# Chunk-selected attention with a squared-ReLU FFN: from single heads with the FFN in blocks to head pairs with the FFN spread in

## The chip, the cores and the metric

The kernel runs on one core of a Trainium2 chip. The metric is the time of one execution on the device, in microseconds (us), lower is better. Engines are named as in the profile: PE is the matrix engine, PEld its weight loads, DVE the vector engine, ACT the scalar engine, POOL the general one, SP the one that issues the stores. PSUM is the memory that PE writes its sums to. The kernel before took 596.76 us (median of the four runs beside which the changed kernel was timed, 593.55 to 600.3).

## The reference

Four batches of 8 heads, 768 positions, 64 columns per head. Keys come in 24 chunks of 32. A query may look at the six chunks with the highest upper bound, which is computed from each chunk's smallest and largest key values, and only backwards. The result of attention, 3072 tokens by 512, goes through an FFN.

```python
k_min, k_max = min and max of k over each chunk of 32
ub = np.sum(np.maximum(q * k_min, q * k_max), axis=-1)      # [.., S, 24]
ub = np.where(causal, ub, -1e9)
top_chunks = np.argsort(ub, axis=-1)[..., -6:]
scores = scale * q @ k.T                                     # masked by chunk and causality
attn = np.exp(scores - max); attn = attn / sum
x = (attn @ v), heads side by side                           # [3072, 512]
h = np.maximum(x @ w_in, 0.0)                                # [3072, 2048]
return h * h @ w_out                                         # [3072, 512]
```

## The kernel before

Work is done head by head. Each head's q and k are transposed on PE; the bounds, the six best and a mask row per chunk are made in steps of 128 queries. The mask rows are appended to q and k (64 + 24 rows), so the score matmul adds the mask. Values go through 65-column matmuls (64 values and a column of ones for the sum), one per 128 queries. The FFN of batches 0 and 1 runs in blocks between the heads of batches 2 and 3; that of batches 2 and 3 runs at the end.

```python
# all weights are loaded first, then q, k, v of a whole batch, as rows of 64 values
nc.gpsimd.dma_start(out=w_in_sb, in_=...)          # ... w_out_sb likewise
nc.gpsimd.dma_start(out=qn, in_=q[b].rearrange("h (j p) d -> p (h j) d", p=128))

def ffn_up(tb, f):                                 # [cut: the loop below is whole]
    ph = psB.tile([128, TOKB], F32, tag="po", name="ph")     # same buffers as the value sums
    for ki in range(NKI):
        nc.tensor.matmul(ph, lhsT=w_in_sb[:, ki, 128*f:128*(f+1)],
                         rhs=xT_sb[:, ki, TOKB*tb:TOKB*(tb+1)], ...)
    # [cut: relu on ACT, square on DVE]
# ffn_down: py from the same psB buffers, 16 matmuls of 512 columns

# per head:
for i in range(NT):                                # bounds and choice, 128 queries at a time
    nc.tensor.matmul(ub_p, lhsT=qr_comb[:, 128*i:128*(i+1)], rhs=kmm, ...)
    nc.vector.tensor_add(ubm, ub_p, ubmask[...])
    nc.vector.max(out=m8, in_=ubm)
    nc.vector.tensor_scalar(selb, ubm, m8[:, 5:6], 0.0, op0=ALU.subtract, op1=ALU.min)
    nc.tensor.matmul(selbT_p[...], lhsT=selb, rhs=ident, is_transpose=True, ...)
nc.scalar.copy(qs_comb[D:KC, :], selbT_p)
for blk in range(NBLK):
    pouts = [psB.tile([128, D + 1], F32, tag="po") for _ in range(3)]
    for j in range(0, i_hi):
        nc.tensor.matmul(ps[:, :w], lhsT=kq_comb[0:KC, ...], rhs=qs_comb[0:KC, qs:q1], ...)
        nc.scalar.activation(e[:, :w], ps[:, :w], ACT.Exp)
        for i in range(max(j, i_lo), i_hi):        # values: 65 moving columns
            nc.tensor.matmul(pouts[ii], lhsT=e[:, col:col+128], rhs=v_aug[:, j, :], ...)
    # [cut: reciprocal of the sum, multiply, per 128 queries]
```

The softmax here doesn't subtract the row's maximum and nothing guards it: scores larger than these inputs give would overflow.

## Time and profile before

| stage of the kernel before | from, to (us) | what it is |
|---|---|---|
| wait | 0 to 32 | q queued behind 4 MB of weights |
| 16 heads without FFN | 32 to 235 | first preparation (to 50 us), then mostly 11.2 us per head, 22.4 per two |
| 16 heads with half of the FFN | 235 to 500 | 16.6 us per head, 33 per two |
| rest of the FFN | 500 to 597 | PE full |

The page of the kernel before: the first PE line is busy us with its share and count of instructions. In the rows by slice each digit stands for a fortieth of the span (14.9 us here), in tenths.

```profile
span 597.3 us, 7719 instructions
...
PE 467.0 (78%) x2592; PEld 227.8 (38%) x2592; DVE 287.6 (48%) x1280; ACT 285.0 (48%) x537; POOL 87.4 (15%) x223
...
PE   0037787787787778787878988789888889999997
...
PEclk9999999999999999955777778777687778999999
```

PE is busy in only 7 to 8 tenths of most slices, and the recorded clock (PEclk) starts at full speed and falls in the second half. The table by windows has the stages; the columns are those of its first line.

```profile
core 0: us, PE busy (x) PEld busy (x) DVE busy (x) ACT busy (x) POOL busy (x), PEclk, DMA share, GB/s
0.00:32.40 32.40, 0.03 (x1) 0.03 (x2) 0.00 (x0) 3.58 (x4) 10.00 (x18) 1.00 1.23 161
32.40:235.00 202.60, 148.50 (x925) 78.86 (x925) 126.94 (x586) 110.38 (x215) 50.56 (x111) 1.00 0.87 41
235.00:500.00 265.00, 224.80 (x1226) 106.31 (x1226) 137.94 (x633) 133.38 (x255) 26.89 (x95) 0.73 0.06 10
500.00:597.30 97.30, 93.71 (x443) 42.62 (x441) 22.77 (x61) 37.65 (x64) 0.00 (x0) 0.99 0.11 44
```

The clock column must be read with care: it shows 1.00 wherever the record of the clock is empty, and here the record begins only at 251 us. There is a second meter in the trace: the mean time of a score matmul of 384 columns. The Trainium skill, "TensorE: Matmul & The Clock Gate", section "Single matmul latency", gives (219 + N)/1.2 ns at the half clock and (398 + N)/2.4 ns at the full one, so for N = 384 an estimate of about 502 and 326 ns. The traces agree: single ones take about 0.50 or 0.33 us; a mean between is a mixture of both. The profile models the ends of matmuls, so the meter was checked against starts: six transposes in a row take 0.85 us in the stage without FFN (at 38.43 us) and 0.52 us after a block of FFN (at 290.75 us). Here is the group in 60 to 80 us and in 320 to 340 us of the kernel before (count, then busy us and mean ns of one):

```profile
L275 PE MATMUL ps<-qs_comb,kq_comb 88*128 88x384 bf16 x10 | 4.8, 508 | 0.0
...
L275 PE MATMUL ps<-qs_comb,kq_comb 88*128 88x384 bf16 x5 | 2.2, 472 | 0.9 <-ACT qs_comb L262 0.9
```

So the whole stage without FFN ran at half clock, whatever the row PEclk says, and even among the FFN blocks most of the attention did (in 20 us windows the mean goes between 389 and 510 ns).

The chain that ended last, and the groups that the change touches (busy us, mean ns; then the idle time before them):

```profile
PE 59%; DVE 16%; ACT 12%; DMA 5%; issue 3%; POOL 3%; ACTq 0%; POOLq 0%; DVEq 0%
...
L289 PE MATMUL po<-vn,e 128*128 128x65 bf16 x672 | 104.5, 242 | 12.0 <-ACT e L280 4.7
L111 PE MATMUL ph<-xT_sb,w_in_sb 128*128 128x512 bf16 x384 | 108.1, 446 | 3.6 <-DVE x_sb L297 3.6
```

PE has 59% of the chain, but DVE and ACT, with their small operations, 28%.

### The profile page before, as it was taken

What the parts mean: (1) busy time and instruction counts of PE and PEld (TensorE: products, weight loads), DVE (VectorE), ACT (ScalarE), POOL (GpSimd) and SP (SyncE); (2) the same over time, 40 slices, a digit from 0 to 9 for tenths busy, and PEclk for the clock granted to TensorE, in tenths of its full rate; (3) what the DMA queues carried; (4) which work ended last, traced back from release to release, by engine and by line L of the source; (5) the groups of instructions that cost most, each with busy time, mean ns of one, the idle gap of its engine ahead of it and who ended that gap; (6) DMA issues with size and microseconds to landing.
All of it is one profiled execution on the core that took longest, in us unless ns stands there. A gap on an engine that the chain in (4) does not pass through costs nothing.

```text
span 597.3 us, 7719 instructions
## 1 busy us (share of the span) xinstructions
PE 467.0 (78%) x2592; PEld 227.8 (38%) x2592; DVE 287.6 (48%) x1280; ACT 285.0 (48%) x537; POOL 87.4 (15%) x223
## 2 busy tenths in 40 slices
PE   0037787787787778787878988789888889999997
PEld 0023343343344334443333434333344434444443
DVE  0036656656755666766555343564327541514040
ACT  2025556455556465555556445554445441526261
POOL 6033114113114112111001011000110110000000
PEclk9999999999999999955777778777687778999999
DMA  7999107909004909000000000000000000010101
GB/s 135 187 147 125 5 2 50 57 0 55 0 1 28 79 2 53 1 2 0 2 0 2 18 36 18 2 0 19 18 36 0 2 1 36 36 53 19 53 19 70
DMA packets 80007, 20.41 MB, mean 34 GB/s; under 512 B 74336, under 2 KB 76384, under 8 KB 79968
## 3 DMA queue, kind: packets, MB, share of 16 engines
q0 software_dynamic: 76512, 13.63, 37.5%
q1 hardware_dynamic: 3456, 6.29, 2.7%
q8 instruction: 20, 0.33, 0.2%
q14 instruction: 19, 0.16, 0.1%
HBM read 27.26 MB, written 6.29 MB: 56 GB/s over the span
## 4 chain that ended last, share of the span: by engine, by line
PE 59%; DVE 16%; ACT 12%; DMA 5%; issue 3%; POOL 3%; ACTq 0%; POOLq 0%; DVEq 0%
PE ph L111 17%; PE py L125 15%; PE ps L275 9%; PE po L289 8%; ACT e L280 7%; DMA kn<-in_k_dram 5%; DVE selb L257 4%; PE kT_p L224 4%; PE qT_p L215 3%; ACT qr_comb L220 2%; DVE ubm L253 2%; DVE x_sb L297 2%; POOL e L282 2%; DVE kmm L232 2%; PE selbT_p L259 2%
## 5 line engine op out<-in xcount | busy, mean ns | idle before, releaser
L280 ACT ACTIVATE e<-ps 128x384 bf16<-128x384 f32 (+2 forms) x288 | 111.6, 418 | 63.2 <-PE ps L275 41.5
L275 PE MATMUL ps<-qs_comb,kq_comb 88*128 88x384 bf16 (+2 forms) x288 | 109.0, 419 | 15.9 <-ACT qs_comb L262 9.1
L289 PE MATMUL po<-vn,e 128*128 128x65 bf16 x672 | 104.5, 242 | 12.0 <-ACT e L280 4.7
L111 PE MATMUL ph<-xT_sb,w_in_sb 128*128 128x512 bf16 x384 | 108.1, 446 | 3.6 <-DVE x_sb L297 3.6
L282 POOL TENSOR_SCALAR_AFFINE_SELECT e<-e 128x128 bf16<-128x128 bf16 x192 | 54.3, 295 | 363.7 <-ACT e L280 362.0
L289 PEld LDWEIGHTS <-e 128*128 128x128 bf16 x672 | 58.4, 118 | 75.1 <-POOL e L282 27.3
L117 ACT ACTIVATE ht<-ph 128x512 bf16<-128x512 f32 x96 | 57.4, 597 | 47.8 <-PE ph L111 46.7
L296 DVE RECIPROCAL recip<-po 128x1 f32<-128x1 f32 x192 | 30.8, 164 | 80.1 <-PE po L289 73.7
L111 PEld LDWEIGHTS <-w_in_sb 128*128 128x128 bf16 x384 | 41.6, 111 | 62.0 <-issue 24.0
L259 PE MATMUL selbT_p<-ident,selb 128*24 128x128 bf16 x192 | 44.3, 260 | 19.2 <-DVE selb L257 11.7
L218 DVE COPY qs_comb<-qT_p 64x768 bf16<-64x768 bf16 x32 | 17.5, 548 | 82.1 <-PE qT_p L215 39.1
L215 PE MATMUL qT_p<-ident,qn 128*64 128x128 bf16 x192 | 25.3, 281 | 39.9 <-DMA qn<-in_q_dram 32.4
L220 ACT ACTIVATE qr_comb<-qT_p 64x768 bf16<-64x768 bf16 x32 | 25.7, 802 | 59.9 <-DVE qr_comb L219 59.5
L134 ACT COPY ob<-py 128x512 f32<-128x512 f32 x24 | 14.1, 586 | 72.8 <-PE py L125 69.9
L262 ACT COPY qs_comb<-selbT_p 24x768 bf16<-24x768 bf16 x32 | 25.0, 780 | 48.1 <-PE selbT_p L259 48.1
L249 PE MATMUL ub_p<-kmm,qr_comb 128*128 128x24 bf16 x192 | 32.3, 189 | 18.7 <-DVE ubm L253 17.0
L297 DVE TENSOR_SCALAR x_sb<-po,recip 128x64 bf16<-128x64 f32 x192 | 45.2, 274 | 1.0
L275 PEld LDWEIGHTS <-kq_comb 88*128 88x128 bf16 x288 | 33.4, 122 | 25.7 <-issue 21.4
L253 DVE TENSOR_TENSOR ubm<-ub_p,ubmask 128x24 f32<-128x24 f32 x192 | 32.1, 185 | 18.0 <-PE ub_p L249 16.2
L224 PE MATMUL kT_p<-ident,kn 128*64 128x128 bf16 x192 | 31.1, 286 | 11.1 <-DVE kmm L232 6.6
L259 PEld LDWEIGHTS <-selb 128*24 128x24 bf16 x192 | 16.5, 92 | 51.4 <-DVE selb L257 36.2
L215 PEld LDWEIGHTS <-qn 128*64 128x64 bf16 x192 | 18.3, 143 | 42.9 <-DMA qn<-in_q_dram 32.4
(699 smaller groups left out, 572.2 us busy)
## 6 DMA issues: line engine op xcount, KB each, us to landing
out_dram<-ob SPq DMA_DIRECT2D x24, 256.0 KB, 2.0
qn<-in_q_dram POOLq DMA_DIRECT2D x4, 768.0 KB, 10.7
kn<-in_k_dram POOLq DMA_DIRECT2D x4, 768.0 KB, 12.2
vn<-in_v_dram POOLq DMA_DIRECT2D x4, 768.0 KB, 10.8
w_in_sb<-in_moe_w_in_dram POOLq DMA_DIRECT2D x1, 2048.0 KB, 13.3
w_out_sb<-in_moe_w_out_dram POOLq DMA_DIRECT2D x1, 2048.0 KB, 21.8
```

The costliest lines, as they stand in the source:

```text
L111: nc.tensor.matmul(ph, lhsT=w_in_sb[:, ki, 128 * f:128 * (f + 1)], rhs=xT_sb[:, ki, TOKB * tb:TOKB * (tb + 1)], start=(ki == 0), stop=(ki ...
L117: nc.scalar.activation(ht, ph, ACT.Relu)
L125: nc.tensor.matmul(py, lhsT=h2state[(tb, f)][:, 128 * t:128 * (t + 1)], rhs=w_out_sb[:, f, :], start=(f == 0), stop=(f == NFI - 1))
L215: nc.tensor.matmul(qT_p[:, 128 * j:128 * (j + 1)], lhsT=qn[:, j, :], rhs=ident, is_transpose=True, start=(j == 0), stop=(j == NT - 1))
L224: nc.tensor.matmul(kT_p[:, 128 * j:128 * (j + 1)], lhsT=kn[:, j, :], rhs=ident, is_transpose=True, start=(j == 0), stop=(j == NT - 1))
L253: nc.vector.tensor_add(ubm, ub_p, ubmask[:, off:off + NC])
L259: nc.tensor.matmul(selbT_p[:, 128 * i:128 * (i + 1)], lhsT=selb, rhs=ident, is_transpose=True, start=(i == 0), stop=(i == NT - 1))
L275: nc.tensor.matmul(ps[:, :w], lhsT=kq_comb[0:KC, 128 * j:128 * (j + 1)], rhs=qs_comb[0:KC, qs:q1], start=True, stop=True)
L280: nc.scalar.activation(e[:, :w], ps[:, :w], ACT.Exp)
L282: nc.gpsimd.affine_select(out=e[:, 0:128], in_=e[:, 0:128], compare_op=ALU.is_ge, fill=0.0, base=0, channel_multiplier=-1, pattern=[[1, 128]])
L289: nc.tensor.matmul(pouts[ii], lhsT=e[:, col:col + 128], rhs=v_aug[:, j, :], start=(not started[ii]), stop=(j == i))
L297: nc.vector.tensor_scalar_mul(x_sb[:, NT * b + i, D * h:D * (h + 1)], pouts[ii][:, 0:D], recip)
```

## The change

Its intent: handle two heads at once so that the small per-128-query operations become wide ones; keep values and sums transposed, so that attention's output needs no transpose before the FFN; load q and k of one pair first, in long packets; and mix the FFN finely into the attention. Values and sums of the two heads go to the two halves of the array (64 columns each). The diff, cut to its core:

```diff
-    nc.gpsimd.dma_start(out=w_in_sb, ...)          # weights first
+    states = {0: load_qk(0)}                       # q and k of pair 0 first, weights with pair 1
+            nc.gpsimd.dma_start(
+                out=t, in_=src[b, 2 * hp:2 * hp + 2].rearrange(
+                    "h (p j) d -> p h j d", p=128))          # rows of 6 x 64 values
 ...
+            nc.vector.tensor_copy(tt.rearrange("d (p j) -> d p j", j=NT),
+                                  pt.rearrange("d (j p) -> d p j", j=NT))   # puts them in order
 ...
+        for i in range(NS):                        # bounds of both heads: block-diagonal kmx, kmn
+            nc.tensor.matmul(ub[:, i], lhsT=qp[:, cols], rhs=kmx[s], start=True, stop=False)
+            nc.tensor.matmul(ub[:, i], lhsT=qm[:, cols], rhs=kmn[s], start=False, stop=True)
+        nc.vector.tensor_add(ubm, ub, ubmask)      # all queries of both heads at once
 ...
-                nc.tensor.matmul(pouts[ii], lhsT=e[:, col:col + 128],
-                                 rhs=v_aug[:, j, :], ...)
+                    rows = slice(D * hh, D * hh + D)
+                    nc.tensor.matmul(av[rows, off:], lhsT=vn[:, hh, j, :], rhs=e[:, off:], ...)
+                    nc.tensor.matmul(den[rows, off:], lhsT=ones, rhs=e[:, off:], ...)
 ...
-            ph = psB.tile([128, TOKB], F32, tag="po", name="ph")
+            ph = psf.tile([128, QB], F32, tag="ff", name="ph")     # own buffers
 ...
+                if j > 0:
+                    values(j - 1)
+                run_ffn(per_step[0])               # one or two FFN units after each score step
+                per_step.append(per_step.pop(0))
 ...
+            nc.scalar.activation(rc, den, ACT.Ln)
+            nc.scalar.activation(rc, rc, ACT.Exp, scale=-1.0)
+            nc.vector.tensor_mul(xT[:, hp, S * b + q0:S * b + q1], av, rc)
```

The FFN of batch b now fills the pairs of batch b + 1; the first four of the 16 pairs have none, and a quarter of the FFN is left for the end.

## The prediction

> **What bounds the kernel now**, by stages of the 597 us execution (windows, chain of waits):
> - 0 to 32 us: the first transpose waits 32.4 us for q, queued behind 4 MB of weights in 256-byte packets.
> - 32 to 235: 16 heads without FFN, 11.2 us each. The page gives clock 1.00, but a 384-column score matmul takes 508 ns, as in the window recorded at 0.50 (505), so I take this stage as cold: the Trainium skill ("TensorE: Matmul & The Clock Gate", the two states) gives 1.2 GHz until the array has been busy for a few us. No engine is full; PE is near its cold limit.
> - 235 to 500: 16 heads, 16.6 us each, with half of the FFN in blocks between heads. The clock swings between 0.50 and 1.00 (mean about 0.72): FFN blocks warm the array, attention cools it.
> - 500 to 597: the other half, PE 100%, 216 ns per 512-column matmul: at its limit.
>
> **What the change does**, per pair of heads (estimates from durations in the trace):
> - PE: value matmuls of 65 columns become wide ones (5376 columns of values, 5376 of sums, 5376 of scores). 9.2 us warm, 17 cold, against 11 and 19. FFN unchanged: 164 us warm in all, 10.2 per pair. PE work hardly falls.
> - DVE: small operations per 128 queries (add 0.18, max 0.18, subtract 0.23, reciprocal 0.16, scale 0.27) give way to wide ones. Two reordering copies from PSUM at about 0.93, four reduces 0.94, ten max 0.18, small copies: 11.5 us against about 18; plus 2 with FFN.
> - ACT: exps 7.5 as before, mask rows and q/k copies gone (6.4), Ln and Exp of the sums added (1.9): 9.4 against 14; 14 with FFN. One table load.
> - The 96 transposes of x vanish.
> - Start: q/k of one pair alone, 1.5 KB packets: about 9 us, not 32, then one exposed preparation of 11.
> - FFN of batch b fills batch b+1: 3/4 rides under attention, 1/4 is tail.
>
> **Sum.** Start 20; four pairs without FFN, 17.5 each (cold PE): 70; twelve with FFN, PE-bound, 19.4 warm, at a mean clock of about 0.78: 25.5 each, 306; tail 2 x 21.7 plus the end: 47. **Predicted 443 us, 395 to 495 in 8 of 10.** Chances: faster by over 2% 0.96, within 2% 0.02, slower 0.02.
>
> **What would show it.** First transpose before 12 us. Pairs without FFN 15 to 20 us apart; with FFN 22 to 29. DVE busy about 230 us, ACT about 235. Clock in the FFN pairs above 0.75, PE over 90% busy there. Tail about 45 us at 216 ns per 512-column matmul. PE over 70% of the chain of waits.
>
> **What would make it wrong.**
> - The clock: if fine mixing keeps PE cold, FFN pairs cost up to 37 us (near 560 in all); if it stays warm, 21 (about 390).
> - Preparation of pair p+1 is one long DVE chain (7 us before the bounds, 2.4 more before the mask transpose). If it stalls PE instead of overlapping with the pair before, add up to 8 us per pair.
> - Sums and values have one PSUM buffer each: Ln, Exp, multiply (about 1.7 us) sit between blocks, twice per pair.
> - Half-array matmuls alternate with full ones. The skill ("TensorEngine Tiling (Array Packing)", Key Properties) says that a mode change drains the array; nothing in this trace prices it. Halves that overlap would save up to a quarter of the value work.
> - Reordering copies might be slower than 0.93 us.

## More of the kernel before

How the clock is lost is seen in the timeline of PE between two blocks (start, length, engine, line, operation, count, and the wait before it):

```profile
283.31 7.15 PE L111 MATMUL ph<-xT_sb,w_in_sb 128*128 128x512 bf16 x20 [0.44 <-DVE x_sb L297]
...
292.00 1.06 PE L259 MATMUL selbT_p<-ident,selb 128*24 128x128 bf16 x4
293.94 0.43 PE L275 MATMUL ps<-qs_comb,kq_comb 88*128 88x384 bf16 x2 [0.87 <-ACT qs_comb L262]
...
295.35 0.33 PE L275 MATMUL ps<-qs_comb,kq_comb 88*128 88x384 bf16 x1
...
295.54 0.50 PE L275 MATMUL ps<-qs_comb,kq_comb 88*128 88x384 bf16 x1
```

The clock has come up during a block of 20 FFN matmuls. Then come 3.5 us of transposes, tiny bound matmuls and waits. The score matmul at 295.35 still takes 0.33 us; the next, at 295.54, takes 0.50. The attention that follows runs at half clock until the next block.

## The result, and the profile after

The changed kernel is correct and took **380.78 us** (median of 4, 379.96 to 381.55) against 596.76 for the kernel before. The ratio is 0.6369, with a 95% interval from 0.6332 to 0.6406. Ratios here are the mean time of one kernel's fast runs over that of the other's of the same rounds, so not quite the ratio of the medians. The direction was right; the time is 62 us under the middle of the prediction and 14 under its lower end.

The page, and the windows of its stages (start; four pairs without FFN; twelve pairs with FFN; tail), with the columns as before:

```profile
span 379.1 us, 6701 instructions
...
PE 347.6 (92%) x2367; PEld 163.3 (43%) x2384; DVE 219.0 (58%) x585; ACT 207.3 (55%) x509; POOL 100.7 (27%) x257
...
PE   1298998799899999999999999999999999999996
...
PEclk9999999957999999999999999999999999999999
```

```profile
0.00:18.20 18.20, 3.82 (x52) 2.92 (x52) 11.30 (x35) 4.31 (x5) 14.77 (x27) 1.00 1.08 108
18.20:88.75 70.55, 64.44 (x387) 27.39 (x387) 44.96 (x114) 36.15 (x91) 24.62 (x62) 0.91 0.64 94
88.75:330.20 241.45, 234.17 (x1701) 110.48 (x1714) 150.74 (x404) 147.10 (x374) 61.29 (x169) 1.00 0.27 40
330.20:379.10 48.90, 45.18 (x233) 22.52 (x232) 12.02 (x33) 19.79 (x39) 0.00 (x0) 1.00 0.11 43
```

PE is now busy in 92% of the span, and 97% of the stage with FFN (234.17 of 241.45 us). The clock meter in 20 to 40, 60 to 80 and 200 to 220 us:

```profile
L277 PE MATMUL ps<-qsc,kqc 88*128 88x384 bf16 x11 | 5.3, 492 | 0.0
...
L277 PE MATMUL ps<-qsc,kqc 88*128 88x384 bf16 x16 | 5.3, 354 | 1.1 <-ACT e L283 0.9
...
L277 PE MATMUL ps<-qsc,kqc 88*128 88x384 bf16 x10 | 2.8, 328 | 0.0
```

The first two pairs ran at half clock (single score matmuls take about 0.50 us until 54.7 us) and the third, from 56 us on, at full (0.32 to 0.34 us). In the fourth the clock fell again, at 76.5 us, and was back at 90.1 us, in the first pair with FFN; from there on all pairs ran at full (326 to 331 ns in every window from 100 us on). The recorded 1.00 before 56 us is again no measurement.

The chain that ended last, and the groups of PE with the reordering copy of DVE:

```profile
PE 75%; POOL 9%; issue 5%; ACT 5%; DMA 4%; DVE 1%; POOLq 0%; ACTq 0%
...
L213 PE MATMUL ph<-xT,w_in_sb 128*128 128x384 bf16 x512 | 103.9, 332 | 2.3 <-ACT ht L218 1.3
...
L269 PE MATMUL den<-e,ones 128*64 128x384 bf16 (+2 forms) x288 | 67.9, 320 | 0.1
...
L266 PE MATMUL av<-e,vn 128*64 128x384 bf16 (+2 forms) x288 | 59.2, 331 | 5.4 <-POOL e L286 3.8
...
L157 DVE COPY kt<-kT 128x768 bf16<-128x768 bf16 x16 | 15.3, 956 | 29.2 <-PE kT L152 29.0
```

The chain is now PE for 75%, and DVE has 1% of it in place of 16. The FFN matmul of 384 columns averages 332 ns, the full clock. The means of the value and sum matmuls in halves (331, 320) mix three widths and, from the first pairs, the half clock. The timeline of one step in which scores of 128 columns are followed by values and sums in halves:

```profile
196.70 0.28 PE L277 MATMUL ps<-qsc,kqc 88*128 88x128 bf16 x2
196.91 0.30 PE L266 MATMUL av<-e,vn 128*64 128x256 bf16 x2
197.04 0.28 PE L269 MATMUL den<-e,ones 128*64 128x256 bf16 x2
197.25 0.39 PE L227 MATMUL py<-w_out_sb,h_2444 128*128 128x512 bf16 x1
```

It is read again beside the fourth experiment. Stage by stage:

| stage | predicted | measured | difference |
|---|---|---|---|
| start, to the first score matmul | 20 | 18.2 | -2 |
| four pairs without FFN | 70 | 70.5 (17.6 each) | +0.5 |
| twelve pairs with FFN | 306 (25.5 each) | 241.5 (20.1 each) | -64.5 |
| tail | 47 | 48.9 | +2 |

So the whole miss lies in one line. Its 25.5 was PE work of 19.4 us at full clock, stretched by a mean clock of 0.78. Work and stage can be set apart: (25.5 - 19.4) x 12 = 73 us were the clock's, and the pairs took 0.7 us more than 19.4, which gives 8 back.

### The profile page after: what moved, and what is told of

It is laid out like the page before. It is cut to its first block, busy times and chain, and to the rows that moved or that the text cites. A ratio compares the mean times of both kernels' runs of the same rounds, so it can differ in the third digit from the quotient of the medians.

```text
span 379.1 us, 6701 instructions
## 1 busy us (share of the span) xinstructions
PE 347.6 (92%) x2367; PEld 163.3 (43%) x2384; DVE 219.0 (58%) x585; ACT 207.3 (55%) x509; POOL 100.7 (27%) x257
## 4 chain that ended last, share of the span: by engine, by line
PE 75%; POOL 9%; issue 5%; ACT 5%; DMA 4%; DVE 1%; POOLq 0%; ACTq 0%
PE ph L213 22%; PE py L227 21%; PE ps L277 10%; PE av L266 9%; PE den L269 8%; DMA w_in_sb<-in_moe_w_in_dram 4%; POOL e L286 2%; POOL vn L76 2%; POOL qn L67 2%; ACT e L283 2%; PE sT L196 2%; POOL kn L67 1%; ACT rc L298 1%; PE kT L152 1%; PE qT L152 1%
## 5 line engine op out<-in xcount | busy, mean ns | idle before, releaser
L213 PE MATMUL ph<-xT,w_in_sb 128*128 128x384 bf16 x512 | 103.9, 332 | 2.3 <-ACT ht L218 1.3
L218 ACT ACTIVATE ht<-ph 128x384 bf16<-128x384 f32 x128 | 62.6, 492 | 39.1 <-PE ph L213 35.5
L277 PE MATMUL ps<-qsc,kqc 88*128 88x384 bf16 (+2 forms) x288 | 76.3, 313 | 4.0 <-ACT e L283 2.9
L269 PE MATMUL den<-e,ones 128*64 128x384 bf16 (+2 forms) x288 | 67.9, 320 | 0.1
L266 PE MATMUL av<-e,vn 128*64 128x384 bf16 (+2 forms) x288 | 59.2, 331 | 5.4 <-POOL e L286 3.8
L277 PEld LDWEIGHTS <-kqc 88*128 88x128 bf16 x288 | 25.9, 99 | 32.0 <-issue 17.1
L269 PEld LDWEIGHTS <-ones 128*64 128x64 bf16 x288 | 25.1, 114 | 27.9 <-issue 23.3
L299 DVE TENSOR_TENSOR xT<-av,rc 128x384 bf16<-128x384 f32 x32 | 17.6, 550 | 30.2 <-ACT rc L298 29.1
L266 PEld LDWEIGHTS <-vn 128*64 128x64 bf16 x288 | 19.8, 113 | 34.4 <-issue 30.8
L157 DVE COPY kt<-kT 128x768 bf16<-128x768 bf16 x16 | 15.3, 956 | 29.2 <-PE kT L152 29.0
L163 DVE TENSOR_REDUCE kmn<-kt 64x24 bf16<-64x768 bf16 x32 | 30.3, 947 | 0.4
L163 DVE TENSOR_REDUCE kmx<-kt 64x24 bf16<-64x768 bf16 x32 | 30.1, 942 | 0.3
L157 DVE COPY qt<-qT 128x768 bf16<-128x768 bf16 x16 | 15.2, 948 | 0.9 <-PE qT L152 0.9
```

What stands on the lines that cost most here:

```text
L157: nc.vector.tensor_copy(tt.rearrange("d (p j) -> d p j", j=NT), pt.rearrange("d (j p) -> d p j", j=NT))
L163: nc.vector.tensor_reduce(dst[rows, hh, :], tt[rows].rearrange("d (c j) -> d c j", j=CH), axis=AX.X, op=op)
L213: nc.tensor.matmul(ph, lhsT=w_in_sb[:, ki, 128 * f:128 * (f + 1)], rhs=xT[:, ki, t0:t0 + QB], start=(ki == 0), stop=(ki == NKI - 1))
L218: nc.scalar.activation(ht, ph, ACT.Relu)
L266: nc.tensor.matmul(av[rows, off:], lhsT=vn[:, hh, j, :], rhs=e[:, off:], start=(j == 0), stop=(j == nj - 1))
L269: nc.tensor.matmul(den[rows, off:], lhsT=ones, rhs=e[:, off:], start=(j == 0), stop=(j == nj - 1))
```

## The experiments

The question is first why the clock holds: is it the spreading of the FFN, or the other form of the attention? Two theories to begin with. One says that the old form of the values (65-column matmuls) is what cooled the array. The other says that it was the FFN in blocks, and that mixing alone warms it. Then the sizes: what half-array matmuls, long packets and the DVE's preparation are worth. Eighteen kernels ran, each beside the kernel before (594 to 599 us).

### 1. The FFN in one block per pair: e1_ffn_blocks

```diff
-                run_ffn(per_step[0])
-                per_step.append(per_step.pop(0))
 ...
         stage_b(p, [1, 2])
+        run_ffn(13)
```

> The new kernel with the 13 FFN units of a pair issued in one block behind the pair instead of one or two after each score step. Theory (the clock): the fine spread is what keeps the array at full clock; in blocks the recorded clock of the FFN pairs falls from 1.00 to about 0.75 and a pair from 20.1 us to 24 to 27, total 425 to 460. Rival (less PE work is all): the same PE work in another order; clock stays above 0.95 and the total within 10 us of 381.

Measured: 405.43 us (median of four, of which two were slow; the two fast ones took 402.89 and 399.74), ratio 0.6705 (0.6659 to 0.6752), pairs with FFN 21.7 us each, score matmul 329 to 332 ns: not cooled. But the experiment did not do what it says. Its timeline inside a pair still shows FFN matmuls (ph) between attention matmuls:

```profile
185.85 0.50 PE L213 MATMUL ph<-xT,w_in_sb 128*128 128x384 bf16 x2
...
186.22 0.32 PE L277 MATMUL ps<-qsc,kqc 88*128 88x384 bf16 x1
...
187.15 0.99 PE L213 MATMUL ph<-xT,w_in_sb 128*128 128x384 bf16 x5
```

Instructions are ordered when the kernel is built, and the FFN has PSUM buffers of its own, so it was mixed in again from its later place in the code. This run doesn't take the mixing away, and was done over as e15.

### 2. The old FFN spread in: e5_before_spread, and only its buffers: e16_before_buffers

e5 is the kernel before with the FFN cut in units that are called after each score step, with sums in the transposes' PSUM buffers:

```diff
-            ph = psB.tile([128, TOKB], F32, tag="po", name="ph")
+            ph = psqk.tile([128, TOKB], F32, tag="qkT_p", name="ph")
 ...  # py likewise, in four parts of 4 matmuls
+            step()                                  # after each score step: some FFN units
```

> The kernel BEFORE with only the FFN spread: its FFN cut into quarters of a down product and single up products, issued one at a time after the score steps instead of in blocks between heads (from the PSUM buffers of the transposes). Theory A (what cools the array is the kind of value work, narrow 65-column matmuls): the recorded clock of the FFN stage stays below 0.85, total 570 to 610. Theory B (spreading alone warms it, although taking the spread out of the new kernel did not cool that one): clock above 0.95 there and a total of 520 to 555.

Measured: 555.26 us, ratio 0.9324 (0.9267 to 0.9381); score matmul in the FFN stage 325 to 327 ns from 280 us on. Spreading alone warms the old kernel, with its narrow values and everything else kept. The time is at the slow edge of what was expected.

e16 changes the buffers alone and leaves the order of the code:

```diff
-            ph = psB.tile([128, TOKB], F32, tag="po", name="ph")
+            ph = psqk.tile([128, TOKB], F32, tag="qkT_p", name="ph")
-            py = psB.tile([128, d_model], F32, tag="po", name="py")
+            py = psqk.tile([128, d_model], F32, tag="qkT_p", name="py")
```

> The kernel BEFORE with one thing changed: FFN sums go into the two PSUM buffers of the transposes instead of the three of the value sums; the order of the code stays, blocks between heads. If buffers alone let the FFN mix in: total 550 to 575 and score matmuls near 330 ns in the FFN stage, as with the fine spread (555). If the order of the code is needed too: 585 to 605, and score matmuls near 450 ns.

Measured: 556.54 us, ratio 0.933 (0.9277 to 0.9383), the same as e5. The window of its FFN stage has a recorded clock of 0.93, against 0.73 in the kernel before. Both figures are too high, since the start of each window lies before the record; by the meter, score matmuls take 325 to 328 ns from 320 us on (361 in one window of seven), where the kernel before has 389 to 510. The timeline shows FFN matmuls in among the mask transposes, just where the old kernel had its gaps:

```profile
235.00:460.00 225.00, 200.11 (x1261) 91.02 (x1261) 136.01 (x615) 131.76 (x260) 27.82 (x96) 0.93 0.09 17
```

```profile
405.71 0.38 PE L111 MATMUL ph<-xT_sb,w_in_sb 128*128 128x512 bf16 x1
406.02 0.23 PE L259 MATMUL selbT_p<-ident,selb 128*24 128x128 bf16 x1
...
406.22 0.38 PE L111 MATMUL ph<-xT_sb,w_in_sb 128*128 128x512 bf16 x1
```

So the FFN of the old kernel stood in blocks because its sums shared three PSUM buffers with the value sums. Two lines of buffer choice are worth 40 us.

### 3. Narrow values in the new kernel: e9_narrow and e10_narrow_blocks

The value and sum matmuls of the new kernel are replaced by the old 65-column form, in the new order. Their outputs are wrong, which doesn't matter for the times. The outputs land in the wrong layout; the work is that of the old form. e10 has e1's edit as well.

```diff
-                    nc.tensor.matmul(av[rows, off:], lhsT=vn[:, hh, j, :], rhs=e[:, off:], ...)
-                    nc.tensor.matmul(den[rows, off:], lhsT=ones, rhs=e[:, off:], ...)
+                    for i in range(max(j, 3 * blk), 3 * blk + 3):
+                        nc.tensor.matmul((av, den)[hh][:, 65 * ii:65 * ii + 65],
+                                         lhsT=e[:, 128 * ii:128 * ii + 128],
+                                         rhs=vn[:, hh, j, :], start=True, stop=True)
```

> The new kernel with its value and sum matmuls in the old form (probabilities as weights, 65 moving columns, 84 per pair instead of 72 half-array ones); WRONG RESULT ON PURPOSE, since x would need transposes that are not there. Theory A (narrow value matmuls cool the array): clock of the FFN stage below 0.85, pair with FFN 23 to 27 us, total 415 to 470. Theory B (the form does not matter, spread FFN keeps it warm): clock above 0.95, pair 20 to 22 us, total 378 to 405.

> The same narrow value matmuls (WRONG RESULT ON PURPOSE) with the FFN in one block per pair, so that both suspected causes of the old cooling are back at once. If either or both together cause it: clock of the FFN stage below 0.8 and total 440 to 500. If the clock still stays above 0.95 (total 400 to 425), the cause lies in neither, but in the waits of the old preparation chain on PE.

Measured: 349.92 us (0.5886, 0.5846 to 0.5927) and 357.81 us (0.6006, 0.5967 to 0.6045); score matmul 326 to 329 ns in the FFN pairs of e9, 18.2 us per pair. Both are faster than either theory said. The narrow form doesn't cool the array: the first theory falls. (e10 has e1's flaw, its FFN could mix in again, so it says nothing about blocks.) It is even cheaper by 1.9 us per pair than the half-array form. (It isn't a kernel: its output would still have to be divided and transposed.)

### 4. Full-array forms of the values: e3_padded and e4_vones

e3 pads the values and the ones with zeros to 128 columns, and both heads add into one full-width sum. e4 puts values and ones of one head side by side, [v | 1], so that one full-width matmul gives both.

```diff
-                    nc.tensor.matmul(av[rows, off:], lhsT=vn[:, hh, j, :], rhs=e[:, off:], ...)
-                    nc.tensor.matmul(den[rows, off:], lhsT=ones, rhs=e[:, off:], ...)
+                    # e3: the weights have 128 columns, zeros in the other head's 64
+                    nc.tensor.matmul(av[:, off:], lhsT=vn[:, hh, j], rhs=e[:, off:], ...)
+                    nc.tensor.matmul(den[:, off:], lhsT=onesw[:, hh], rhs=e[:, off:], ...)
+                    # e4, in its place: the weights are [v | 1] or [1 | v]
+                    nc.tensor.matmul((av, den)[hh][:, off:], lhsT=vn[:, hh, j], rhs=e[:, off:], ...)
```

> The new kernel with values and ones padded with zeros to 128 columns, both heads accumulating into the whole array: no half-array matmuls in values and sums, hence no overlap of halves, and no change of array mode around them. Theory: overlap of halves saves 2.2 us per pair at full clock and mode changes cost about 1.5; total within 395 to 405 if mode changes cost nothing, 380 to 392 if they cost 1.5 us per pair. Rival (halves do not overlap in effect): total at or below 381.

> The new kernel with values and ones side by side as one 128-column weight per head: value and sum from one full-array matmul, the same array time as two overlapped halves, no mode change, one Ln and one multiply more per block of queries. Theory (mode changes cost about 0.17 us per score step, 1.5 us per pair): 350 to 368. Rival (mode changes cost nothing that matters): 378 to 384. Between this run and the padded one the array time differs by 2.2 us per pair at full clock, so by about 30 us if PE is the limit.

Measured: e3 369.48 us (0.6173, 0.6155 to 0.619), e4 369.43 us (0.616, 0.6121 to 0.6198). e3 was expected slower than the change and is faster: missed. e4 lies just over its range. The step shown above, in e4 (scores of 128 columns, one value matmul per head, next FFN):

```profile
180.21 0.28 PE L280 MATMUL ps<-qsc,kqc 88*128 88x128 bf16 x2
180.32 0.27 PE L272 MATMUL av<-e,vset 128*128 128x256 bf16 x1
180.43 0.27 PE L272 MATMUL den<-e,vset 128*128 128x256 bf16 x1
180.54 0.81 PE L220 MATMUL ph<-xT,w_in_sb 128*128 128x384 bf16 x4
```

Two halves do overlap: in the changed kernel the two value matmuls of 256 columns take 0.13 us (196.91 to 197.04), one full-width one here 0.11. "TensorE: Matmul & The Clock Gate" says so in its Part 3 ("multiple matmuls concurrently in the same array"), and this trace agrees. But from the first score matmul to the first value matmul it is 0.21 us there and 0.11 here, and from the sums to the next full-width matmul 0.21 us there, of which the sums need 0.13. So a change between halves and full width costs about 0.10 us on the way in and 0.08 on the way out; an estimate for a pair, with both in each of its 9 steps, is 1.6 us. "TensorEngine Tiling (Array Packing)", section Key Properties, says that a change of mode drains the array; these gaps fit it, but no run separates the drain from the loading of the weights.

What e4 takes off PE isn't all gained. In the stage with FFN its PE is busy for 218.0 us against 234.2 in the changed kernel (16 less), but the stage is only 5 us shorter: idle time of PE grows from 7 to 18 us. Over 100 to 320 us, the waits of score matmuls for the exps grew from 0.4 to 5.7 us. The rest of e4's gain, and all of e3's, lies in the first four pairs, which end at 74.5 us (e3) and 83.9 us (e4) instead of 88.75; e3's array is first warm 30 us sooner (at 26 us by the record; 382 ns in 20 to 40 us). e3's pairs with FFN take 20.4 us, no less than the 20.1 of the changed kernel.

### 5. Useless matmuls in the first four pairs: e2_fill6

Six matmuls of 384 columns on constants after each score step of the first four pairs, 54 per pair.

```diff
+                if p < NP:
+                    fill(p, 6)
```

> The new kernel with six useless 384-column matmuls after each score step of the first four pairs (54 per pair, 8.6 us of PE per pair at full clock, 17 at half). Theory: these four pairs (17.6 us each) run cold, at half clock, although the record says 1.00; the useless work warms the array, score matmuls of 384 columns fall from about 500 to about 330 ns, and the four pairs take no longer than before, perhaps 14 to 17 us each: total 366 to 382. Rival (the recorded clock of 1.00 is right, and PE work is the limit there): each pair grows by about 8 us, total 405 to 415.

Measured: 377.67 us, ratio 0.6311 (0.6293 to 0.6329). The clock meter in 20 to 40 us of this run:

```profile
L286 PE MATMUL ps<-qsc,kqc 88*128 88x384 bf16 x16 | 5.1, 329 | 0.0
```

It is 329 ns from the start, against 492. The four pairs end at 86.6 us, against 88.75, with an estimated 8.6 us of added work per pair (54 times 0.16 us, the step from one 384-column matmul to the next in the rows of e4 above: four in 0.81 us, the last of which takes 0.33): the added work was free, because the clock that it brought paid for it. That shows that the first pairs of the changed kernel are cold at their start, as predicted, whatever the row PEclk says.

### 6. Blocks that can't mix: e15_true_blocks

e1's edit, and the FFN sums in the buffers of values and sums, so that the FFN of a pair can't start before its attention is through with them.

```diff
-            ph = psf.tile([128, QB], F32, tag="ff", name="ph")
+            ph = psav.tile([128, QB], F32, tag=("av", "den")[f % 2], name="ph")
 ...  # py likewise; run_ffn(13) after the pair, as in e1
```

> The new kernel with the FFN behind each pair, as in the first of these runs, and with the FFN sums in the PSUM tiles of values and sums instead of two of their own, so that FFN matmuls cannot slip in between attention matmuls as they did there (the timeline of that run shows it). Theory (mixing FFN finely into attention, by the code or by buffers of its own, is what keeps the array warm and PE filled): mean of 384-column score matmuls in the FFN stage at 390 ns or more (326 warm, 503 cold), recorded clock there below 0.85, a pair 26 to 31 us, total 460 to 520. Rival (the new attention keeps the array warm by itself): score matmuls below 350 ns; time still rises, to 425 to 460, by the lost overlap alone.

Measured: 414.53 us median (400.14 to 415.25). Three of the four runs, the profiled one too, were slow, so there is no ratio; the one fast run took 400.14. The pairs with FFN take 21.8 us each in the profiled run, 1.7 more than in the changed kernel; this stage is at full clock in that run. The fast run has no trace, so its 19.4 us over the changed kernel can't be shared out among the stages; its mean clock of 0.991 leaves no room for a cold FFN stage either. The clock meter, in 40 to 60 us and in 160 to 180 us:

```profile
L277 PE MATMUL ps<-qsc,kqc 88*128 88x384 bf16 x13 | 6.2, 502 | 0.0
...
L277 PE MATMUL ps<-qsc,kqc 88*128 88x384 bf16 x9 | 3.0, 333 | 0.2 <-ACT e L283 0.2
```

In the profiled run the array is cold until 105.6 us, but for 3.4 us (mean clock 0.962); whether that is what makes it slow isn't shown, since its first four pairs end within 0.5 us of those of the changed kernel. Its pairs with FFN are warm without any mixing (331 to 335 ns). So mixing isn't what keeps the new kernel's clock: its attention, in stretches of 9.4 to 10.6 us between blocks without one FFN matmul, holds it alone. That isn't so for any length of time: in the fourth pair of the changed kernel, at 76.5 us and without FFN matmuls around it, the clock fell 20 us after it had come up. Nor does mixing by itself pay for the 1.7 us per pair: e1, which mixes from its later place in the code, takes 21.7 us as well. The windows of 20 to 60 us and 140 to 180 us say one more thing:

```profile
20.00:60.00 40.00, 38.53 (x209) 15.64 (x206) 27.60 (x65) 20.56 (x53) 15.56 (x38) 1.00 0.92 141
140.00:180.00 40.00, 37.70 (x285) 19.05 (x284) 30.21 (x84) 25.44 (x61) 12.34 (x30) 1.00 0.35 44
```

PE is as busy in the cold window (38.5 of 40 us) as in the warm one (37.7). The busy share doesn't tell the state. This attention doesn't quickly bring a cold array to full clock, but it does bring it: the clock came up at 105.6 us, before the first FFN matmul at 107.5.

### 7. Gaps put back: e17_blocks_gaps and e18_spread_gaps

Why does the new attention hold the clock when the old one lost it? One PSUM buffer for the scores instead of two makes each score matmul wait for the exp before. e17 does this to e15, e18 to the changed kernel.

```diff
-    pss = ctx.enter_context(tc.tile_pool(name="pss", bufs=2, space=PSUM))
+    pss = ctx.enter_context(tc.tile_pool(name="pss", bufs=1, space=PSUM))
```

> As e15 (FFN behind each pair, unable to mix), with one PSUM buffer for the scores instead of two: each score matmul must wait for the exp of the one before, so PE has a gap of about 0.5 us per score matmul inside the attention. Theory D (what keeps the array at full clock in e15 is that its attention leaves PE few gaps): the 384-column score matmul in the pairs with FFN goes up from the 331 to 335 ns of e15 to more than 420 ns on average, and these pairs cost 31 to 36 us each, about 540 to 590 us in all. Rival E (something else in the new attention, such as its wide value matmuls, keeps the array warm): the score matmul stays at 325 to 345 ns, and the pairs cost only the added waits, 27 to 31 us each, 480 to 540 us in all.

> The changed kernel with one PSUM buffer for the scores, FFN mixed in as it was. Control for e17: the FFN fills the same gaps. Theory D: score matmul at 325 to 345 ns in the pairs with FFN, which cost 21 to 26 us each, and the first four pairs, which have no FFN, stay cold (about 500 ns) and cost 22 to 27 us each; 430 to 480 us in all. Rival E says the same for the pairs with FFN; if the score matmul is cold there too, mixing in FFN work isn't enough to hold the clock when the attention has gaps.

Measured: e17 484.42 us (0.8129, 0.8054 to 0.8204), 26.9 us per pair with FFN; e18 415.73 us (0.6983, 0.6933 to 0.7032), 22.2 us per pair. e18's score matmul stays at 327 to 330 ns from 120 us on, and the time is under the 430 to 480 expected; its first pairs were at 409 to 447 ns in 20 to 80 us, less cold than the 500 expected. e17 falls between its two theories, nearer to rival E (the time and the price of a pair are at the low end of E's ranges): in ten of the sixteen 20 us windows from 100 us on the score matmul is at 323 to 328 ns, in the other six at 362 to 454. One such dip, in e17's timeline:

```profile
214.66 0.32 PE L277 MATMUL ps<-qsc,kqc 88*128 88x384 bf16 x1 [0.18 <-ACT e L283]
...
215.89 0.50 PE L277 MATMUL ps<-qsc,kqc 88*128 88x384 bf16 x1
```

After gaps and transposes the score matmul at 215.89 takes 0.50 us, where that at 214.66 took 0.32. With gaps the unmixed kernel loses the clock now and then, which e15 and e18 don't from 106 us on; but it doesn't sink to the old kernel's level.

The kept traces allow a closer look. The clock record changes in steps of 3.41 us. For each step the columns that matmuls and transposes stream were added up, at about 0.42 ns per column at full clock (512 columns follow each other in 216 ns in the tail) and twice that at half, as a share of the step (an estimate; the two halves are each counted in full). In the kernel before, the clock fell after 13 steps that were filled to 14 to 33%, and stayed up after 45 that were filled to 41% or more; it rose after 14 steps of 88% or more. In the stretches of e15 without FFN every whole step was filled to 54% or more. In all twenty traces 64 of 77 falls followed a step below 42%, and only 7 of 1688 steps that kept the clock were below it. The last two steps at full clock after the old kernel's block shown above (PE's busy time by the profile, ends modelled, is the first figure after the length); after the second the clock is lost:

```profile
288.72:292.13 3.41, 3.41 (x28) 1.84 (x26) 2.56 (x13) 1.72 (x3) 0.00 (x0) 1.00 0.00 0
292.13:295.55 3.42, 1.66 (x14) 0.82 (x13) 0.72 (x6) 1.83 (x4) 0.62 (x3) 1.00 0.00 0
```

So gaps go with the loss in the old kernel and in the new, and e17, which puts them back, brings some of the loss back. Which parts of the new attention close them isn't taken apart. The skill's clock page says in Part 4 that a transpose doesn't count as PE-busy in the same way, and the two dips shown here and in the kernel before do follow transposes. But the counts fit better with the transposes in: without them 47 of the 1688 steps would be below 42%, and the changed kernel's clock came up at 90.1 us after a step with only 40% in matmuls and 27 transposes. No run takes transposes alone away.

### 8. The choice late, in blocks: e11_choice_late_blocks

Bounds and choice per 128 queries, directly ahead of the pair's scores, as in the old kernel; e1's edit as well.

```diff
-        ub = pst.tile([128, NS, 2, NC], F32, tag="tp", name="ub")
 ...
+    def choose(p):                                  # called at the start of stage_b
+        for i in range(NS):
+            ub = pss.tile([128, 2, NC], F32, tag="ps", name="ub")
 ...          # add, two max, compare, transpose per 128 queries
```

> The new kernel with the choice of chunks done per 128 queries (bound matmul, add, max, compare, transpose in turn, through the score buffers) directly ahead of the scores of the same pair, as the kernel before does, and the FFN in blocks per pair. Theory (the old cooling comes from PE waiting inside attention, between FFN blocks, for a chain that alternates with DVE): 384-column score matmuls in the FFN stage rise from 326 to above 400 ns on average, recorded clock below 0.85, total above 440. Rival (still something else in the old kernel): score matmuls stay at about 330 ns and the total below 430.

Measured: 441.76 us (0.7414, 0.7372 to 0.7456), 23.2 us per pair with FFN. The score matmul is mostly at 332 ns, with dips (528, from two matmuls, in 240 to 260 us): the time is that of the theory, the clock that of the rival. So the clock explains little of the 3.1 us per pair over the changed kernel, of which e1's edit alone accounts for 1.6; the exposed chain of small operations is left as the likely cause of the rest. Another 21 us went before the end of the fourth pair (110 us against 89). Since the FFN could still mix (see e1), it doesn't decide on the clock.

### 9. Weights first again: e6_weights_first

```diff
+    nc.gpsimd.dma_start(out=w_in_sb, ...)           # and w_out_sb
     states = {0: load_qk(0)}
 ...
-        if p == 1:
-            load_weights()
```

> The new kernel with the 4 MB of weights loaded ahead of everything, as before. Theory (the start term): first transpose at about 27 us instead of 5.0, total 400 to 410. Rival (queues share the engines evenly, order hardly matters): total below 390.

One run, whose state is unknown: 396.1 us, with 20.0 us per pair with FFN as before, and the first transpose at 25.9 us. The order of the loads is worth about 15 us (396.1 less 380.78), a little less than the 400 to 410 us that was expected.

### 10. Short packets: e7_short_packets

q and k loaded as rows of 256 bytes again, with a plain copy in place of the reordering one.

```diff
-                    "h (p j) d -> p h j d", p=128))
+                    "h (j p) d -> p h j d", p=128))
-            nc.vector.tensor_copy(tt.rearrange("d (p j) -> d p j", j=NT),
-                                  pt.rearrange("d (j p) -> d p j", j=NT))
+            nc.vector.tensor_copy(tt, pt)
```

> The new kernel with q and k loaded row by row in 256-byte packets, as before, so that the copy out of PSUM needs no reordering. Theory (loads are prefetched two pairs ahead, so packet length shows only in the first load; the reordering copy of 0.95 us falls to about 0.7): first transpose 1 to 3 us later, DVE 5 to 8 us less busy in all, total within 5 us of 381. Rival (long packets carry a real part of the gain): total above 390.

Measured: 360.31 us, ratio 0.6039 (0.6 to 0.6078): 20 us faster than the change. Missed. The copy of this run:

```profile
L157 DVE COPY kt<-kT 128x768 bf16<-128x768 bf16 x16 | 8.9, 558 | 39.0 <-PE kT L152 35.3 <-PE qT L152 3.5
```

It takes 558 ns against 956 (the line L157 of the changed kernel above): the reordering costs 0.4 us twice a pair. A load of 192 KB lands after 4.8 us instead of 4.5, and the first transpose starts at 5.69 us instead of 4.96, so long packets gave 0.7 us, once. The pairs with FFN take 19.3 us each instead of 20.1, which fits two copies. The first four pairs end at 75.2 instead of 88.75 us. That is more than eight copies explain; the array was first warm some 20 us sooner (356 against 453 ns in 40 to 60 us) and stayed so. Why it was sooner stays open.

### 11. Twice the reduces: e8_double_reduce

The four reduces of the keys are done twice, 3.8 us of DVE per pair.

```diff
-                for op, dst in ((ALU.max, kmx[s]), (ALU.min, kmn[s])):
+                for op, dst in ((ALU.max, junk), (ALU.min, junk),
+                                (ALU.max, kmx[s]), (ALU.min, kmn[s])):
```

> The new kernel with the four min/max reduces of a pair run twice (3.8 us more DVE per pair, 60 us in all, in the middle of the preparation chain). Theory (PE is the limit, the preparation of the next pair hides behind the current one): exposed once at the start (+3.8) and a little in the first four pairs; FFN pairs still about 20.1 us; total 382 to 395. Rival (the preparation chain is exposed in each pair, as I feared in the prediction): +3.8 per pair, total 430 to 445.

Measured: 410.57 us (0.689, 0.685 to 0.6929); pairs with FFN 22.0 us each. Of 3.8 us added, 1.9 show in the time: between the two theories. Time added to the preparation is half exposed, although DVE is busy for only 58% of the changed kernel's span.

### 12. Together: f2_vones_fill_short, f3_vones_short, f4_padded_short

f2 is e4 with e7's edit and three useless matmuls per step in the first four pairs; f3 is e4 with e7's edit and a fourth value buffer; f4 is e3 with the same.

```diff
+                    # f2, f3: lhsT = [v | 1]   f4: zero-padded values and ones
+                    "h (j p) d -> p h j d", p=128))
+            nc.vector.tensor_copy(tt, pt)
+                if p < NP:                          # f2 only
+                    fill(p, 3)
```

> A version meant to beat both: values and ones in one 128-column weight, three useless matmuls after each score step of the first four pairs to keep the array warm, short packets with plain copies. The first four pairs should take 12 to 14 us each instead of 17.6, pairs with FFN 19 to 19.7: total 345 to 358. If the fill does not warm the array at half the amount: 362 to 370.

> Candidate to beat both: short packets with plain copies, values and ones in one 128-column weight, no fill, four buffers of v instead of three. First four pairs about 12.5 us each, FFN pairs 19: total 347 to 356. If the extra Ln and multiply outweigh the saved mode changes: 357 to 362.

> Second candidate: short packets with plain copies, zero-padded values and ones (whole array, twice the columns, no more DVE or ACT work). First four pairs 11.5 to 12 us, FFN pairs 19.3 to 19.8: total 352 to 360. With the one before: if columns of PE work are the limit, this one is slower by 20 us or more; if the preparation on DVE is, they are within 6 us.

Measured, five rounds each: f2 **356.29 us** (0.598, 0.595 to 0.6011), f3 360.55 us (0.6049, 0.6016 to 0.6083), f4 370.82 us (0.6217, 0.619 to 0.6244). All correct. f2 is the best kernel here that gives the right result, 24 us under the change; its pairs with FFN take 19.0 us. f3 came out in the range of its second case, and f4 missed its range by 11 us. f4 needs 0.9 us more per pair with FFN than f3, for 5376 more columns on PE, an estimated 2.2 us (0.16 us per 384 columns): neither PE nor the preparation alone is the limit.

## Why the prediction was right or wrong

- **"Start 20"**, measured 18.2: right. q and k of one pair come first; e6, in its one run, prices it at 15 us.
- **"four pairs without FFN, 17.5 each (cold PE): 70"**, measured 70.5: right, and mostly for the reason given: e2 shows that they were cold at the start. That a part of them was warm (56.0 to 76.5 us) changed little in the sum; e15's four, nearly all cold, took 70.6 us too.
- **"tail 2 x 21.7 plus the end: 47"**, measured 48.9: right.
- **"twelve with FFN, PE-bound, 19.4 warm, at a mean clock of about 0.78: 25.5 each, 306"**: this step failed. PE was busy for 97% of the stage, but the clock was 1.00 in place of 0.78, and the pair took 20.1 us. The 0.78 seems to be carried over from the old kernel's 0.72 to 0.73 in its FFN stage ("FFN blocks warm the array, attention cools it"), as if any attention cooled the array; the prediction names no other source. It belonged to the old attention standing alone between blocks: e16 ends that by two lines of buffers, and the score matmul goes from 389 to 510 ns down to 325 to 328; and e15 shows that the new attention alone between blocks doesn't cool (331 to 335 ns). The prediction did name the case ("if it stays warm, 21 (about 390)") under what would make it wrong, and put its range's lower end at 395; that case came true with 20.1.
- The mechanism that one would tell first, that fine mixing keeps the array warm, isn't the reason in the new kernel. It warms the old one (e5, e16), but e15 shows the new one warm without it. The reason is that its attention leaves fewer gaps: e17 shows it in part (with gaps put back it dips in six of sixteen windows, where e15 doesn't), and the count of steps in section 7 agrees; that its fewer small steps are what closes the gaps is argued.
- **The 19.4** held within 0.7 us, in part by luck: it left out things that work against each other, and whether they make up the sum isn't shown. Halves overlap, which the prediction counted only as a chance ("up to a quarter of the value work"); mode changes cost some 1.6 us a pair (an estimate from two timelines), and of time added to the DVE's preparation half is exposed (e8), so that it isn't hidden as "PE-bound" supposed.
- **"Two reordering copies from PSUM at about 0.93"**, measured 0.95 to 0.956: right, but their use was not asked. They were taken for part of the bargain with long packets; e7 shows that the bargain loses 20 us.

- **The smaller signs**: first transpose at 4.96 us ("before 12"), PE 75% of the chain ("over 70%"), DVE busy 219 us ("about 230"), tail at 48.9 ("about 45"): right. ACT was busy for 207 us and not "about 235".

## What to carry to other kernels

Before carrying a clock from one stage or kernel to the next, measure it by the length of one fixed matmul in small windows, and ask what the engine does in the microseconds between dense blocks: busy share and the recorded clock may both mislead. Where a filler can't mix, look for the buffer that it shares with what it should fill. Price each part of a bundled change by undoing it alone: here one part of a change that gained 36% lost 20 us.

## What the Trainium skill lacked or had wrong

- "TensorEngine Tiling (Array Packing)": Key Properties names the drain at a mode change without a price. Here it is about 0.10 us from full width to 64-column halves (0.21 against 0.11 us) and 0.08 us back (0.21 against 0.13), weight loads included. Full-width [v | 1] weights, without these changes, took 0.4 us less per pair with FFN (19.7 against 20.1).
- "TensorE: Matmul & The Clock Gate", Part 3 has no case of two 64-column halves with all 128 rows. Here two matmuls of 256 columns in halves took 0.13 us where one at full width took 0.11.
- The same page, Part 1, describes an idle and a busy window, and oscillation with short idle times, but gives no share of work at which the clock changes. Here, in the kernel before, it fell after steps of 3.41 us filled to 14 to 33% and stayed after 41% or more (section 7); and with PE busy 96% of a 40 us window by the profile the array stayed at half clock (496 to 502 ns per score matmul), where with 94% it stayed at full (331 to 335 ns).
- The same page warns that clock events in a trace are unreliable, but doesn't name the case met here: the record is empty before its first event, and the profile's row then shows 1.00, while score matmuls of 384 columns took 498 to 508 ns for 200 us. From the first event on, record and meter agree here.
- The same page, Part 4, on transposes: the counts of section 7 fit better when transposes are work like any other (the changed kernel's clock came up at 90.1 us after a step with 40% in matmuls and 27 transposes). No run tests it alone.
- "DMA: Bandwidth & Descriptors", Specifications, asks for at least 512 bytes per transfer for line rate. That isn't contradicted, but the page has no measured landing time of one load at two lengths of row: here a load of 192 KB landed after 4.8 us with rows of 256 bytes, and after 4.5 with rows six times as long.
